# Loading the weights of an attention and MLP kernel in transfers of 88 and 40 partitions instead of 128

## The chip, the cores and the metric

The kernel runs on one core of a Trainium2 chip. The metric is device time in microseconds (us) of one execution; lower is better. The kernel before takes 523.25 us, the median of two runs (522.9 and 523.61).

## The reference

A delta-rule attention of 4 batches, 8 heads, 768 steps and head size 48 is followed by a layer norm and a two-layer MLP (384 to 1536 to 384) with a residual. All inputs are float32.

```python
# q, k, v: (4, 8, 768, 48); beta: (4, 8, 768)
k_n = k / (np.linalg.norm(k, axis=-1, keepdims=True) + 1e-06)
for t in range(S):
    y[:, :, t] = q[:, :, t] @ state                     # per batch and head
    v_old = k_n[:, :, t] @ state
    state += beta[t] * outer(k_n[:, :, t], v[:, :, t] - v_old)
x = y.transpose(0, 2, 1, 3).reshape(4, 768, 384)        # heads side by side
xn = (x - mean) / sqrt(var + 1e-06) * g_ln
out = x + maximum(xn @ w_ch1, 0) @ w_ch2                # (384, 1536), (1536, 384)
```

The MLP's weights reach the kernel as 64-bit floats, seen as pairs of 32-bit words. The kernel turns them into float32 itself: per weight it scales the high and the low word and adds them.

## The kernel before, in words

The sequence is cut into 12 chunks of 64 steps, each for all 32 batch-head pairs. Within a chunk the recurrence becomes matrix products with the inverse of a 64 x 64 triangular matrix. For the first chunk this inverse is made by doubling on TensorE (PE), in `first_inverse` (from line 711): five rounds, each with products E (line 770) that VectorE (DVE) merges (line 775), products Z (line 786), DVE transposes of Z (line 735), and copies of Z back into the tile `xt` on ScalarE (ACT), line 729. Round n's Z waits for the `xt` copies of round n-1. Later chunks take another way (`rows_inverse`), prepared beside the work on the chunk before. The MLP of a chunk is interleaved with the recurrence of the next one: lines 1406 and 1448 or 1426 for the first chunks, lines 1307 and 1523 (a scheme of seven products) from then on.

The weights come in 12 pieces of 128 partitions x 1536 words (768 KB). `fetch` (line 568) loads one piece in two transfers of 384 KB, each 128 partitions x 3 runs of 1 KB, both issued from ACT's queue through the helper `dma` (line 407), so that all issues have line 410. A piece lands in one of five buffers: three tiles `words`, and the two halves of `h_all`, a tile that the MLP needs only later. `convert` (line 579) is an ACT scaling of the high words (line 592), a DVE shift (line 597), an ACT scaling of the low words (line 600) and a GpSimd (POOL) addition (line 610) into `w1_sb` or `w2_sb`.

The order of the work is written out. Every operation is recorded as a numbered step; the text `ORDER` (line 156) lists the steps, `emit` (line 101) issues them in that order, and `in_this_order` (line 25) keeps it on each engine. So each engine carries out a fixed sequence, and an instruction that waits holds up all that follow on its engine. A transfer issued from ACT stands in ACT's sequence among its copies.

The two hardware queues for transfers, SP's and ACT's, share eight completion counters, which the framework hands out in turn to the transfers of both in the order of `ORDER`. An issue waits until the transfer that had its counter before it, eight transfers earlier, has landed. So at most eight transfers of SP and ACT together are in flight. Numbering the transfers from 0, those around the start of the weights are: 9 `kr` and 10 `beta_b`, 11 `v`, 12 `tb`, 13 and 14 `tb` (q), 15 `v`, 16 `kr` (all SP), 17 to 22 weights (ACT), 23 `gd` and 24, 25 `gb` (SP), 26 to 29 weights (ACT), and then again SP's.

Of the kernel before, what the change touches and what calls it, by code (L numbers as in the profile page):

```python
# [53 lines left out]
class Line:  # L54
# [14 lines left out]
    def add(self, eng, cost, fn, r=(), w=(), name="", after=(), **plan):  # L69
        s = Step()  # L70
        s.eng, s.cost, s.fn, s.n, s.name, s.plan = eng, cost, fn, len(self.steps), name, plan
        s.out = w[0] if w else None
        s.opens, s.shuts = [], []
        for k in (*r, *(k for k in w if k in self.unread and k not in r)):
            if k in self.writer:
                self.writer[k].opens.append(k[:2])
                s.shuts.append(k[:2])
        self.unread.difference_update(r)
        self.unread.update(w)
        s.key = f"{self.tag} {eng} {name or next(k if isinstance(k, str) else k[0] for k in w)}"  # L80
        deps = set()
        if eng == "ACT" and "bulk" not in plan and "table" in self.writer:
            deps.add(self.writer["table"])
        for k in r:
            if k in self.writer:
                deps.add(self.writer[k])
        for k in (*w, *after):
            if k in self.writer:
                deps.add(self.writer[k])
            deps.update(self.readers.get(k, ()))  # L90
        for k in r:
            self.readers.setdefault(k, []).append(s)
        for k in w:
            self.writer[k] = s
            self.readers[k] = []
        deps.discard(s)
        s.deps = deps
        self.steps.append(s)
        return s
# [158 lines left out]
def kernel(  # L258
# [13 lines left out]
    nc = tc.nc  # L272
# [98 lines left out]
    add = line.add  # L371
# [18 lines left out]
    def half(e):  # L390
        return slice(C * e, C * e + C)
# [15 lines left out]
    def dma(eng, out_, in_, n, ns, r=(), w=(), **kw):  # L407

        cost = 0.65 if eng != "SP" else 0.45 if n <= 512 else 0.62
        add(eng, cost, lambda: QUEUE[eng].dma_start(out=out_, in_=in_), r, w, bulk=n * ns / 16e3, np=n, **kw)  # L410
# [14 lines left out]
    for i in (2, 1):  # L425
# [6 lines left out]
            out=ident, in_=ident, compare_op=ALU.not_equal, fill=1.0, base=0, pattern=[[-1, 128]], channel_multiplier=1  # L432
# [20 lines left out]
    for n in MASKED:  # L453
        k_, m, w = min(n, 4) if n == 6 else n, masks[n] if n < 6 else mask4, C if n < 6 else BK
# [3 lines left out]
                out=t1, in0=xor[:, 0:w], scalar1=w - 1, scalar2=k_, op0=ALU.bitwise_and, op1=ALU.logical_shift_right  # L458
# [6 lines left out]
                out=t2, in0=own, scalar1=k_, scalar2=1, op0=ALU.logical_shift_right, op1=ALU.bitwise_and  # L465
# [5 lines left out]
                out=m, in0=t1, scalar=1, in1=t2, op0=ALU.is_equal, op1=ALU.mult  # L471
# [20 lines left out]
    for e in range(2):  # L492
        c_pool(
            lambda e=e: nc.gpsimd.affine_select(
                out=pmask[half(e)], in_=pmask[half(e)], compare_op=ALU.is_gt, fill=0.0, base=0,
# [69 lines left out]
    BUF = [3, 4, 0, 1, 2, 0, 1, 2, 0, 1, 2, 0]  # L565
    RUN = 128

    def fetch(i, after=(), **kw):
        dst = words[BUF[i]].rearrange("p n w -> p (n w)").rearrange("p (b a x) -> p a b x", a=2, x=2 * RUN)
        src = pieces[i][1]  # L570
        if len(src.shape) == 2:
            src = src.rearrange("p (a n) -> p a n", a=2)
        for a in range(2):
            dma(
                "ACT", dst[:, a], src[:, a].rearrange("p (b x) -> p b x", x=2 * RUN), 384, 54,
                w=[("wd", BUF[i], a)], after=after, **kw,
            )

    def convert(i, c0=0, n=WN, **kw):

# [1024 lines left out]
    for i in range(5):  # L1605
        fetch(i, pr=-70 + i, after=["keys in"])
# [14 lines left out]
    for c0 in (0, 384):  # L1621
        for i in range(3):
            convert(i, c0, 384, pr=-50 if c0 == 0 else -10)
    fetch(5, pr=-55)
    for i in range(3, 6):
        convert(i, pr=2)
# [27 lines left out]
    for i in range(6, len(pieces)):  # L1654
        fetch(i, pr=i)
        convert(i)
    for i in (2, 3):
        add(
            "Pool", 1.0, lambda i=i: nc.gpsimd.memset(xts[i], 0.0), [], [("xz", i)], pr=20,
            after=[("xt", i, 0), ("xt", i, 1)],  # L1660
# [91 lines left out]
```

## Time and profile before

| | |
|---|---|
| median of two runs | 523.25 us |
| profiled execution | 520.78 us, its span from first to last instruction 519.1 us |
| granted TensorE clock, mean | 0.982 |
| PE busy | 487.1 us (94% of the span) |
| DVE, ACT, POOL busy | 360.8, 206.9, 280.3 us |
| chain that ended last | PE 79%, DMA 5%, SP's queue 3%, issue 3%, DVE 3%, ACT 3% |
| weight transfers | 24 of 384 KB, issued from 10.1 to 83.7 us |
| issue to landing of one, min, median, max | 3.5, 4.5, 7.3 us into `words`; median 7.0 us into `h_all` |

The page gives the busy time of each engine, the span in 40 slices, the chain of work that ended last, and groups of instructions by line. A name like ACTq or SPq is the issuing part of that engine. The timeline lists instructions in order of time: start, duration, engine, line, operation, tiles, count, and in brackets how long the engine had stood idle and what ended that. "issue" is time for which the profile shows no wait. Beside these views the trace has the moments at which a transfer's 16 shares report to its counter; the 16th is its landing.

### The profile page before, as it was taken

How to read it: one execution, taken by the hardware profiler on the slowest of the kernel's cores; microseconds unless marked ns; L12 is line 12 of the kernel's file. 1: busy time of each engine (PE TensorE's matmuls, PEld its weight loads, DVE VectorE, ACT ScalarE, POOL GpSimd, SP SyncE). 2: the span in 40 equal slices, each digit the busy share in tenths (PEclk: the TensorE clock that was granted, in tenths of full speed). 3: DMA queues.
4: the chain of work that ended last, by engine and by line, in shares of the span. 5: the costliest groups of instructions: out<-in, count | busy, mean ns of one | idle time of the engine just before them, and what ended most of it. 6: DMA issues, size and time to landing. Idle time of an engine off the chain costs nothing.

```text
span 519.1 us, 22785 instructions
## 1 busy us (share of the span) xinstructions
PE 487.1 (94%) x9972; PEld 448.9 (86%) x9972; DVE 360.8 (70%) x814; ACT 206.9 (40%) x462; POOL 280.3 (54%) x447
## 2 busy tenths in 40 slices
PE   5577888999899999999999999999999999999997
PEld 4466786768798889999999989999999999999996
DVE  6577739798887567988889986757988446244241
ACT  5587845423431333234242632533513514424130
POOL 3435654604554877976764274473453742564554
PEclk9878998999999999999999999999999999999999
DMA  9957876585515866345853356643404403003011
GB/s 135 294 115 204 191 154 178 107 195 95 90 26 141 156 134 109 68 88 141 167 120 55 83 108 157 132 81 66 102 10 111 104 17 93 4 1 100 2 39 30
DMA packets 181635, 54.56 MB, mean 105 GB/s; under 512 B 164888, under 2 KB 177312, under 8 KB 181536
## 3 DMA queue, kind: packets, MB, share of 16 engines
q1 hardware_dynamic: 168512, 40.10, 37.9%
q10 hardware_dynamic: 10816, 9.83, 6.6%
q0 software_dynamic: 2208, 3.17, 3.8%
q8 instruction: 78, 1.28, 1.0%
q14 instruction: 21, 0.17, 0.1%
HBM read 36.30 MB, written 16.78 MB: 102 GB/s over the span
## 4 chain that ended last, share of the span: by engine, by line
PE 79%; DMA 5%; SPq 3%; issue 3%; DVE 3%; ACT 3%; POOL 2%; ACTq 0%; DVEq 0%; POOLq 0%
PE f L1523 27%; PE f L1307 22%; PE f L1426 6%; PE f L1448 3%; SPq L410 3%; PE two L819 3%; PE by L1033 2%; PE two L1033 2%; PE by L1095 2%; DMA xnt<-xld 2%; PE two L1088 2%; PE f L1406 1%; PE two L1105 1%; DMA words<-in_moe_w_ch_dram 1%; DMA gb<-gd 1%
## 5 line engine op out<-in xcount | busy, mean ns | idle before, releaser
L1510 POOL TENSOR_TENSOR h_all<-h_all 128x256 f32<-128x256 f32 x99 | 72.7, 745 | 30.5 <-PE f L1523 13.8
L1523 PE MATMUL f<-w_sb,h_all 128*128 128x192 f32 x396 | 82.2, 331 | 1.0 <-ACT h_all L1334 0.6
L1523 PE MATMUL f<-words,h_all 128*128 128x192 f32 x396 | 76.7, 329 | 0.0
L1523 PEld LDWEIGHTS f<-w_sb,h_all 128*128 128x128 f32 x396 | 65.1, 190 | 3.0 <-ACT h_all L1334 1.6
L1330 DVE TENSOR_TENSOR h_all<-f,h_all 128x512 f32<-128x512 f32 x72 | 48.9, 685 | 26.4 <-PE f L1307 19.3
L1523 PEld LDWEIGHTS f<-words,h_all 128*128 128x128 f32 x396 | 65.0, 190 | 1.5 <-issue 0.5
L1548 POOL TENSOR_TENSOR words<-h_all 128x128 f32<-128x128 f32 x66 | 31.2, 491 | 63.4 <-ACT h_all L1334 30.4
L907 DVE TENSOR_TENSOR tmp<-xb,gb 128x31 f32<-128x31 f32 (+19 forms) x139 | 57.5, 413 | 3.9 <-POOL xb L894 0.3
L1325 ACT COPY h_all<-f 128x512 f32<-128x512 f32 x45 | 26.2, 586 | 82.4 <-PE f L1307 68.8
L914 DVE TENSOR_TENSOR xb<-xb,tmp 128x31 f32<-128x31 f32 (+19 forms) x139 | 52.6, 378 | 3.7
L410 POOL DMA_DIRECT2D tb<-in_k_dram x64 | 42.2, 662 | 0.3 <-POOL tb L1630 0.3
L1334 ACT ACTIVATE h_all<-h_all 128x512 f32<-128x512 f32 x54 | 32.7, 626 | 23.9 <-DVE h_all L1330 23.5
L1307 PE MATMUL f<-x_new,w_sb 128*128 128x128 f32 x288 | 40.3, 278 | 0.1
L1307 PE MATMUL f<-xnt,w_sb 128*128 128x128 f32 x288 | 40.2, 277 | 0.0
L1307 PEld LDWEIGHTS f<-x_new,w_sb 128*128 128x128 f32 x288 | 36.5, 191 | 0.6 <-issue 0.2
L1307 PEld LDWEIGHTS f<-xnt,w_sb 128*128 128x128 f32 x288 | 36.5, 192 | 0.6 <-issue 0.2
L1541 DVE TENSOR_TENSOR o<-f,x 128x192 f32<-128x192 f32 x33 | 11.4, 352 | 36.8 <-PE f L1523 30.9
L1426 PE MATMUL f<-xnt,w_sb 128*128 128x256 f32 x144 | 34.5, 387 | 1.4 <-issue 1.4
L1426 PEld LDWEIGHTS f<-xnt,w_sb 128*128 128x128 f32 x144 | 26.4, 190 | 5.4 <-issue 1.8
L1523 PE MATMUL f<-w_sb,words 128*128 128x192 f32 x132 | 26.3, 329 | 0.0
L682 POOL TENSOR_TENSOR v<-v,kpair 128x768 f32<-128x768 f32 x10 | 14.7, 1473 | 14.0 <-DVE pt L897 14.0
L610 POOL TENSOR_TENSOR w_sb<-words 128x768 uint32<-128x768 uint32 (+1 forms) x11 | 14.7, 1348 | 13.7 <-ACT words L600 10.2
(239 smaller groups left out, 983.4 us busy)
## 6 DMA issues: line engine op xcount, KB each, us to landing
words<-in_moe_w_ch_dram ACTq DMA_DIRECT2D x20, 384.0 KB, 4.5
gd<-gsb SPq DMA_DIRECT2D x11, 512.0 KB, 3.9
v<-in_v_dram SPq DMA_DIRECT2D x24, 192.0 KB, 4.2
kr<-in_k_dram SPq DMA_DIRECT2D x46, 96.0 KB, 3.4
out_dram<-o SPq DMA_DIRECT2D x46, 96.0 KB, 2.2
xld<-xlt SPq DMA_DIRECT2D x9, 384.0 KB, 2.4
xnt<-xld SPq DMA_DIRECT2D x36, 96.0 KB, 2.9
tb<-in_q_dram SPq DMA_DIRECT2D x40, 64.0 KB, 2.8
```

The lines of the kernel that those rows point to most:

```text
L410: add(eng, cost, lambda: QUEUE[eng].dma_start(out=out_, in_=in_), r, w, bulk=n * ns / 16e3, np=n, **kw)
L907: lambda j=j, n=n, w=w, t=t: nc.vector.tensor_tensor(out=t, in0=xv[:, 0:n, j : j + 1].to_broadcast([128, n, w]), in1=gv[:, j : j + 1, j + ...
L914: "DVE", dve(n * w), lambda t=t, rest=rest: nc.vector.tensor_tensor(out=rest, in0=rest, in1=t, op=ALU.subtract),
L1033: nc.tensor.matmul(dst[half(e), hp, j], src[drows(hp), (e if n else key_half(c, hp, e)) * GP + j], s_all[drows(hp), e, j], start=(n == 0 o ...
L1307: nc.tensor.matmul(wide(p[:, f : f + 128]), w[:, f : f + 128], r, start=start and i == 0, stop=True, skip_group_check=True)
L1325: add("ACT", act(512), lambda: nc.scalar.copy(o, p), pk, ok)
L1330: add("DVE", dve(512), lambda: nc.vector.tensor_tensor(out=o, in0=x, in1=y, op=op), [*xk_, *yk], ok)
L1334: add("ACT", act(512), lambda: nc.scalar.activation(o, o, ACTF.Relu, scale=scale), [], ok)
L1426: nc.tensor.matmul(p[:, 0:TOK], w1_sb[:, t, f * 128 : (f + 1) * 128], xnt[:, t], start=(t == 0), stop=(t == KC - 1))
L1510: add(eng, cost, lambda: e.tensor_tensor(out=out_, in0=x, in1=y, op=op), r, w, port=2 if eng == "Pool" else 1, pr=-2)
L1523: lambda f=f, t=start and f == order[0]: nc.tensor.matmul(p[:, 0:D2], lhs(f), rhs[:, f], start=t, stop=(f == order[-1]), skip_group_check=True
L1548: lambda f=f + i: e.tensor_tensor(out=s3[f], in0=one(0, 0)[0](f), in1=one(1, 0)[0](f), op=ALU.subtract),
```

## The change

Each of the 24 weight transfers is issued as two, partitions 0 to 87 and partitions 88 to 127, one right behind the other on ACT's queue. Bytes, runs, buffers, the recorded steps and `ORDER` stay as they are: one step now issues two transfers.

```diff
+        def go(a):
+            for r in (slice(0, 88), slice(88, 128)):
+                nc.scalar.dma_start(out=dst[r, a], in_=src[r, a].rearrange("p (b x) -> p b x", x=2 * RUN))
+
         for a in range(2):
-            dma(
-                "ACT", dst[:, a], src[:, a].rearrange("p (b x) -> p b x", x=2 * RUN), 384, 54,
-                w=[("wd", BUF[i], a)], after=after, **kw,
-            )
+            add("ACT", 1.3, lambda a=a: go(a), after, [("wd", BUF[i], a)], bulk=384 * 54 / 16e3, np=384, **kw)
```

The cost (1.3) and the other numbers given to `add` were for a planner and do not act here, since the order is written out. Each of the 48 transfers takes a counter in turn, so from the first weights on each transfer up to the last weights has another counter and another predecessor than before; behind the last weights the turn is the same again, since 24 is a multiple of eight.

## The prediction

> **What bounds the kernel now.** I read the page first, then a table by stretches, then the chain and ACT's timeline over the time in which weights are issued (10.1 to 83.7 us).
>
> ```profile
> PE   5577888999899999999999999999999999999997
> q10 hardware_dynamic: 10816, 9.83, 6.6%
> q8 instruction: 78, 1.28, 1.0%
> words<-in_moe_w_ch_dram ACTq DMA_DIRECT2D x20, 384.0 KB, 4.5
> h_all<-in_moe_w_ch_dram ACTq DMA_DIRECT2D x4, 384.0 KB, 7.0
> ```
>
> The first seven slices of 13 us are the only ones in which PE is not full, and weights move only there. What is lost there moves all that follows; nothing behind can take it back, since each engine's order is fixed.
>
> ```profile
> 10.00:30.00 20.00, 13.54 (x411) 11.46 (x413) 11.03 (x23) 12.50 (x32) 5.86 (x10) 0.81 0.98 231
> 30.00:50.00 20.00, 15.55 (x600) 13.44 (x596) 15.79 (x40) 15.18 (x34) 10.89 (x15) 0.84 0.77 172
> 100.00:519.00 419.00, 410.52 (x7750) 383.98 (x7742) 293.41 (x627) 143.75 (x315) 232.93 (x380) 1.00 0.43 89
> ```
>
> Columns are length, busy time of PE, PE's weight loads, DVE, ACT, POOL, granted clock, share of the DMA engines, GB/s. From 10 to 30 us the DMA engines are full (0.98) while no computing engine is: this is the inverse of the first chunk, one short operation after another. From 100 us on PE works 410.52 of 419 us.
>
> The chain of work in that stretch, start, duration and what:
>
> ```profile
> 20.65 0.69 PE two L770 x30
> 21.34 0.38 PE by L628 x2
> 21.72 2.54 issue
> 24.26 1.54 PE by L628 x6
> 25.80 1.96 PE f L786 x64
> ```
>
> PE stands still for 2.54 us although no wait is recorded, and only then does round 2's product Z (line 786, 25.80) come. This product needs the copies into `xt` that ACT makes meanwhile:
>
> ```profile
> 17.53 0.50 ACTq L410 DMA_DIRECT2D h_all<-in_moe_w_ch_dram  x1
> 17.71 0.20 ACT L674 COPY knat<-knrm 64x8 f32<-64x8 f32 x1
> 18.73 0.37 ACT L729 COPY xt<-f 128x256 f32<-128x256 f32 x1 [0.82 <-DVE qt L735]
> 19.08 0.38 ACTq L410 DMA_DIRECT2D h_all<-in_moe_w_ch_dram  x1
> 19.55 0.74 ACT L729 COPY xt<-f 64x256 f32<-64x256 f32 x2 [0.45 <-DVE qt L735]
> 20.69 0.75 ACT L729 COPY xt<-f 64x256 f32<-64x256 f32 x2 [0.39 <-DVE qt L735]
> 21.25 0.38 ACTq L410 DMA_DIRECT2D words<-in_moe_w_ch_dram  x1
> 21.46 0.37 ACT L729 COPY xt<-f 64x256 f32<-64x256 f32 x1
> ```
>
> The copies end at 21.83, so they have 25.80 - 21.83 = 3.97 us to spare. Weight issues stand between them. The waits of SP's queue show that an issue does wait for its counter's earlier transfer:
>
> ```profile
> SPq L410 <- DMA words<-in_moe_w_ch_dram: 12.0, 6, 2.7
> ```
>
> **The change, part by part.** It removes nothing. It adds 24 issues on ACT's queue and gives the transfers of both queues other predecessors, as the turn of eight goes faster. Times below are on the profile's own scale; that execution took 520.78 us, 2.5 below the median of 523.25, and I add the difference in time to the median.
>
> *Issue time.* Weight issues one behind the other start 0.42 and 0.54 us apart (16.57, 16.99, 17.53), so an added one costs ACT's queue about 0.45, all 24 about 11 us. What counts is where a copy that the chain needs stands behind it.
>
> *First piece, 10.05 us.* The copy of `kt` (line 633) that starts at 10.51, right behind the issue, comes 0.45 later, and through the product of line 695 (11.66) the whole chain to 17.17. The next two issues stand before gaps of ACT (0.79 us at 14.31). The second of 14.43 has transfer 14 (`tb`) before it, landed at 16.29 by its counter; its issue ends at 16.7, where the copy behind it started at 16.6. Value **+0.45**, already spent inside the spare time of the next step.
>
> *`h_all`, the step that matters.* Before, the three issues at 16.57, 16.99 and 17.53 had transfers 12 to 14 before them, all landed by 16.29. Now they are six. The first gets the counter of transfer 15 (`v`, issued 10.21, to landing 9.2 us in the view of that tile, so 19.42), the second that of 16 (`kr`, landed 20.06 by its counter), the others those of the first two pieces. ACT's queue stands until 19.42, issues the second at 20.06, and four more at 0.45: the first `xt` copy starts at about 22.0 instead of 18.73. Behind it stands the fourth `h_all` transfer, now two, with the counters of the second and third of those six, issued at 20.1 and 20.5. To landing I take 5 us, between the page's median of 4.5 and the 5.9 of the fastest into `h_all`: 25.1 and 25.5. The second is issued by 25.9, the remaining five copies take 1.9 us without a gap (0.74 + 0.75 + 0.37; DVE's transposes are long done), and they end at 27.9. Z of round 2 starts there instead of at 25.80: **+2.1**. PE's standstill of 2.54 us is cover here; without it Z could have started at 23.3 (25.80 - 2.54), and these waits would cost 4.6. From below: `v` and `kr` land 0.8 and 1.0 us earlier, since the `h_all` transfers no longer compete with them, and the landings take the smallest of 3.5 us: copies end near 25.2, nothing lost. From above: 8.1 us, the most into `h_all`: end near 31, +5.2.
>
> *First `words1` piece, 29.14 and 29.55 us.* Two issues become four; behind them stands an `xt` copy on which round 3's Z waits (line 786 at 30.94, released by ACT's line 729). Their predecessors (a weight transfer, `gd`, two `gb`) have landed by then with the same shift. **+0.9**; between 0.8 and 1.1 by the two distances above.
>
> *SP's queue.* `gd`, `gb`, `kr` now have the weights of 14.43 to 29.55 before them. The last `gb` waits for the last part of `words1`, issued near 33 and landed near 38 to 39; before it waited until 36.12. The same 3 us, not added to the others: `kr` behind it is needed at 43.79, by which time PE is that much later too.
>
> *The other 16 added issues* (42.47 to 83.70 us). By my walk along the turn their predecessors have landed; the nearest is `tb` under the issue at 43.83, less than 2 us early. ACT has gaps there (1.59 us at 48.80, 0.85 at 50.12, 1.0 to 1.6 us five times from 69 to 80) and runs behind PE. I take **+0.3**, for the four at 42 to 45 us, where ACT has little rest. Bounds: 0, and 16 x 0.45 = 7.2 if every gap were on the chain.
>
> *Bandwidth.* No byte is added. A transfer of `words` issued alone lands after 3.5 us, so from both sides: nothing, or what the rival on fewer engines gives.
>
> The Trainium skill's page "DMA: Bandwidth & Descriptors", under "Rules for kernel authors", advises against two transfers to disjoint partition halves: they share the same engines and serialize. By that rule the split brings nothing to set against the issues, as the sum has it; no run so far shows it.
>
> **Sum**: 2.1 + 0.9 + 0.3 = 3.3 us, so 523.25 + 3.3 = **526.5 us**, 0.6% slower.
>
> **The rivals.**
> *Fewer engines.* 88 and 40 partitions may not spread over all 16 engines. A packet takes 6.6% x 16 x 519.1 us / 10816 = 51 ns; over 16 engines a transfer is 24 packets (1.2 us) each, if 88 run on eleven engines with 8 partitions each and 40 on ten with 4 (both divide so), 12 partitions and 36 packets on the busiest (1.8 us). With four to five pairs ahead of the landing that the fourth `h_all` transfer waits for, it comes 0.6 x 4 = 2.5 us later: 529. For it: the engines are full from 10 to 30 us. Against: while ACT stands, less is in flight.
> The same page, under "Why a DMA increments its semaphore by 16 and not by 1", states that a transfer uses the largest number up to 16 that divides its slowest dimension, hence 11 and 10, the lowest-numbered. By it the sum would be 529 in the crowd; the trace of before, with all its transfers in multiples of 16, cannot show it.
>
> *Faster: PE's standstills go.* PE stands 2.54 us (21.72) and 1.72 us (83.95) on the chain with no wait shown, both while weights are in flight, and q8 moves 78 blocks of 16 KB (1.28 MB / 78) of instructions. If those queue behind weight packets and the split leaves the engine that brings them free, both standstills can go, and landings come early. The first saves nothing unless the `xt` copies are also ready; so 523.25 - 1.7 + 0.9 + 0.3 - up to 1.5 (waits resolved by 24.3) = about 521 to 523. Against: the bound of 25.2 on the copies leaves 0.6 at most. It decides if round 2's Z starts before 25.
> The Trainium skill, "Runtime: NRT & Kernel Launch", section "Instruction fetch mechanics", has sequencers refill in 16 KB blocks over a DMA queue, mostly hidden; the block size agrees with q8, the standstills speak against "hidden".
>
> *Hidden.* Landings are quick and the 3.97 us of spare cover the wait: 0.9 + 0.3, 523.5 to 524.5.
>
> *A wait chain.* One late landing in the turn of eight holds ACT, whose next issues are the predecessors of the next: SP and ACT wait for each other through 50 us. For it: SP already loses 12 us to weights. With the upper bounds, 5.2 + 1.1 + some 3 of the 7.2: 532 and more.
>
> **How the numbers follow.** Forecast (524.5 to 528) 0.50; fewer engines (528 to 531) 0.18; hidden 0.13; faster 0.11; wait chain 0.08. The range 522 to 531 leaves out the wait chain and half of "faster". A measurement of this kernel tells about 2% (10.5 us) from no change: slower beyond 533.7 is part of the wait chain, 0.05; faster beyond 512.8 needs more than all standstills, 0.01; within 0.94.
>
> **What would show it.** In ACT's timeline six `h_all` issues, the first near 19.4, then a standstill until two more near 25, with `xt` copies of line 729 behind them near 22 and 26; Z of line 786 near 28; four `words1` issues in a row. From 100 us on everything moved by one constant. Wrong would be: `h_all` issues not waiting, a shift that grows behind 50 us, or Z before 25.

## The result, and the profile after

The changed kernel takes **531.39 us** (median of two runs, 531.12 and 531.67) against 523.25: 8.1 us more, a ratio of **1.0156 [1.0112, 1.0199]**. That is within the 2% that tells a change from none by the yardstick used here, but above the forecast of 526.5 and just above the range of 522 to 531. Here and below a ratio leaves out executions over 1.5% above the fastest of their kernel, and is not the quotient of the two medians.

The profiled execution took 531.67 us (span 530.0), 10.9 more than that of before. These two numbers differ from the medians because single executions of one and the same kernel scatter by about 1% here (before: 517 to 529 us in all batches together), and the profile of before shows one of the quicker ones. So shifts between two profiles are read below only with other profiles of the same arrangement beside them.

The page of the changed kernel (lines of code are one higher than before), in this order: PE's busy share in 40 slices, the queue of the weights, the queue of instructions, the weight transfers, and the chain's shares by engine:

```profile
PE   4757698899989999999999999999999999999997
q10 hardware_dynamic: 10936, 9.83, 7.3%
q8 instruction: 78, 1.28, 1.1%
words<-in_moe_w_ch_dram ACTq DMA_DIRECT2D x20, 264.0 KB
PE 71%; DMA 9%; DVE 4%; POOL 4%; ACT 4%; issue 3%; SPq 3%; ACTq 2%; DVEq 0%; POOLq 0%
```

Bytes are the same (9.83 MB), packets nearly so. What is new is in the last line: ACT's issuing part holds 2% of the chain, 0% before, and transfers 9% instead of 5%. In the slices the loss again lies in the first eight. The table by stretches (columns as before):

```profile
10.00:30.00 20.00, 13.48 (x306) 11.35 (x306) 9.15 (x20) 7.66 (x20) 5.86 (x10) 1.00 0.97 182
30.00:50.00 20.00, 15.55 (x515) 13.86 (x516) 13.54 (x31) 16.41 (x39) 7.86 (x11) 0.67 0.79 142
100.00:519.00 419.00, 413.36 (x7996) 384.74 (x7995) 299.11 (x637) 151.44 (x331) 233.24 (x377) 1.00 0.43 91
```

From 10 to 30 us ACT works 7.66 us instead of 12.50: it stands. The granted clock is 1.00 there and 0.81 before, so the clock is not the reason. ACT's timeline around the `h_all` issues shows what it stands for:

```profile
19.71 5.37 ACTq L575 DMA_DIRECT2D h_all<-in_moe_w_ch_dram  x6
25.18 0.37 ACT L730 COPY xt<-f 128x256 f32<-128x256 f32 x1 [6.41 <-DMA h_all<-in_moe_w_ch_dram]
27.79 1.40 ACTq L575 DMA_DIRECT2D h_all<-in_moe_w_ch_dram  x2
29.29 0.74 ACT L730 COPY xt<-f 64x256 f32<-64x256 f32 x2 [3.73 <-DMA h_all<-in_moe_w_ch_dram]
29.67 0.30 ACTq L575 DMA_DIRECT2D words<-in_moe_w_ch_dram  x1
30.05 1.14 ACT L730 COPY xt<-f 64x256 f32<-64x256 f32 x3
```

Six issues in a row, the first at 19.71; ACT's copies idle 6.41 us before the first `xt` copy; then 3.73 us more behind the second group. PE's timeline has the other end of it:

```profile
25.36 0.88 PE L629 MATMUL by<-ident,tb 128*128 128x128 f32 x6 [0.46 <-issue]
30.90 2.42 PE L787 MATMUL f<-xt,gsb 64*64 64x64 f32 x64 [4.66 <-issue]
```

Round 2's Z starts at 30.90 (25.73 before), behind a standstill of 4.66 us.

To see at which place the time goes, I follow one and the same ACT instruction through all profiles: how much later than in the profile of before it starts, for instructions that stood at 43, 80 and 100 us there and for one near the end.

| us later than in the profile of before | at 43 | at 80 | at 100 | at 505 |
|---|---|---|---|---|
| the change | 6.5 | 13.7 | 11.5 | 10.8 |
| the change, another execution | 6.6 | 12.4 | 9.8 | 11.8 |

From 100 us on the shift stays within 2 us, as forecast. But only about half of it is there at 43 us; the rest comes between 43 and 80 us, where the forecast had 0.3 us. A shift that grows behind 50 us is one of the signs that the prediction itself named as wrong: from 50 to 80 us it goes from 6.6 to 13.7 us, and from 8.0 to 12.4 in the other execution.

Two theories come out of this. **Front**: the turn of the eight counters, with the six issues behind `v` and `kr`. **Late**: something in the 14 later transfers, either the time of their issues on ACT's queue, or slower landings because 88 and 40 partitions use fewer engines. The experiments take the two places apart, then the causes within each.

### The profile page after: what moved, and what is told of

Same layout as the page of the kernel before. It is cut to its first block, busy times and chain, and to the rows that moved or that the text cites. A ratio compares the mean times of both kernels' runs of the same rounds, so it can differ in the third digit from the quotient of the medians.

```text
span 530.0 us, 22834 instructions
## 1 busy us (share of the span) xinstructions
PE 492.7 (93%) x9972; PEld 455.2 (86%) x9972; DVE 362.1 (68%) x814; ACT 206.6 (39%) x462; POOL 279.8 (53%) x447
## 3 DMA queue, kind: packets, MB, share of 16 engines
q10 hardware_dynamic: 10936, 9.83, 7.3%
## 4 chain that ended last, share of the span: by engine, by line
PE 71%; DMA 9%; DVE 4%; POOL 4%; ACT 4%; issue 3%; SPq 3%; ACTq 2%; DVEq 0%; POOLq 0%
PE f L1524 26%; PE f L1308 22%; PE f L1427 6%; DMA words<-in_moe_w_ch_dram 4%; PE two L820 3%; SPq L410 3%; PE f L1449 2%; ACTq L575 2%; PE by L1034 2%; PE two L1089 2%; PE by L1096 2%; PE two L1034 2%; PE two L1106 1%; DMA gd<-gsb 1%; DMA gb<-gd 1%
## 5 line engine op out<-in xcount | busy, mean ns | idle before, releaser
L1335 ACT ACTIVATE h_all<-h_all 128x512 f32<-128x512 f32 x54 | 32.8, 626 | 24.0 <-DVE h_all L1331 23.8
L1308 PE MATMUL f<-xnt,w_sb 128*128 128x128 f32 x288 | 40.3, 278 | 0.0
L1542 DVE TENSOR_TENSOR o<-f,x 128x192 f32<-128x192 f32 x33 | 11.5, 351 | 35.4 <-PE f L1524 30.0
L1407 PE MATMUL f<-xnt,w_sb 128*128 128x128 f32 x144 | 21.4, 312 | 3.6 <-ACT h_all L1415 3.6
```

What stands on the lines that cost most here:

```text
L1308: nc.tensor.matmul(wide(p[:, f : f + 128]), w[:, f : f + 128], r, start=start and i == 0, stop=True, skip_group_check=True)
L1335: add("ACT", act(512), lambda: nc.scalar.activation(o, o, ACTF.Relu, scale=scale), [], ok)
L1407: nc.tensor.matmul(p[:, 0:128], w1_sb[:, t, f * 128 : (f + 1) * 128], xnt[:, t, cols], start=(t == 0), stop=(t == KC - 1))
```

## The experiments

Every ratio is against the kernel before, run beside it (523.58, 523.35 and 523.59 us in the three groups), with its 95% interval.

### The changed kernel once more

No edit; it stands beside `first`, `last` and `s8048`.

> The changed kernel itself (88 and 40 partitions everywhere), for an interval and as the yardstick beside the other three. Every theory: 1.5% slower than before, 530 to 532 us; in the profile round 2's product Z (line 787) near 31 us instead of 25.8, everything behind 100 us moved by 9 to 11 us.

Measured: 532.93 us, **1.0202 [1.0107, 1.0296]**, a little above what was expected. Together with the first measurement the change costs 1.6 to 2.0%. This and what follows is the yardstick for the parts.

### Splitting only the first five pieces, only the last seven

```diff
-            for r in (slice(0, 88), slice(88, 128)):
+            for r in (slice(0, 88), slice(88, 128)) if i < 5 else (slice(0, 128),):    # "first"
+            for r in (slice(0, 88), slice(88, 128)) if i >= 5 else (slice(0, 128),):   # "last"
```

The first five pieces are the ten transfers up to 36 us, the last seven the 14 from 42 us on.

> Only the first five pieces split (10 added issues, all before 40 us), the other seven as before. Theory 'two places': the front loses 5 to 6 us by ACT standing for counters and the late issues lose 3 to 4 on their own, so 528 to 529.5 us here, with Z of round 2 near 31. Rival 'one place': all of it is lost in the front and the later growth follows from it: 531 us. Rival 'given back': the shift of the front is absorbed by 60 us, and the loss is the late issues': 523 to 525 us.

> Only the last seven pieces split (14 added issues, from 42 us on), the first five as before. Theory 'two places': nothing moves before 42 us, then the added issues on ACT's queue cost 2.5 to 4 us, 526 to 527 us. Rival 'one place': 523 to 524 us. Rival 'given back': 530 to 531 us.

Measured: first **1.0071 [1.0018, 1.0124]**, last **1.0101 [1.0058, 1.0144]**. Each costs something; the sum, 1.7%, is what the whole costs. So there are two losses in two places that add up, and the late one, which I had put at 0.3 us, is about as large as the front (late 5.3 us by its ratio and 3.0 by the difference of the medians of the group, front 3.7 and 3.2). The median of `last`, 526.56 us, is where "two places" had it; that of `first`, 526.82, is below its 528 to 529.5, so the front costs less than the 5 to 6 us expected.

Where the late one arises shows in the chain of `last`, followed back through the time of its late issues (start, duration, what; steps of up to 0.05 us left out):

```profile
76.22 0.47 ACTq L575
76.69 0.43 issue
77.11 0.80 ACTq L575
77.96 0.07 ACT nrm_b L884
78.07 0.31 ACTq L575
78.39 0.56 issue
78.95 0.80 ACTq L575
79.80 0.28 ACT h_all L1415
...
84.41 0.80 ACTq L575
85.24 0.84 ACTq L575
86.11 0.80 ACTq L575
86.96 0.29 ACT h_all L1415
```

The chain runs from issue to issue on ACT (L575), with ACT's short copies between them; an issue that lies on it whole takes 0.80 to 0.84 us. PE waits for these copies: its products of line 1407 follow at 81.90 and 87.29. In `first`, whose late transfers are whole, the chain of the same stretch belongs to PE's products, and no issue is on it:

```profile
77.20 1.44 PE f L945 x84
78.65 2.88 PE f L1407 x24
81.52 1.39 PE by L950 x103
82.91 2.90 PE f L1407 x24
```

### The second part of the late transfers issued from SP

```diff
+            for r in (slice(0, 88), slice(88, 128)) if i >= 5 else (slice(0, 128),):
-                nc.scalar.dma_start(out=dst[r, a], ...)
+                (nc.sync if r.start else nc.scalar).dma_start(out=dst[r, a], ...)
```

The 14 late transfers are split as in `last`, with the same counters in the same turn and the same sizes. Only who issues the 40-partition part differs.

> Only the last seven pieces split, at 88 and 40, but the 40-partition part is issued from SP's queue, so that ACT has as many issues as before; the turn of counters and the engines used stay as in the run with both parts on ACT (526.6 us). Theory 'issue time on ACT's queue': the loss of 3 us goes, 523 to 524.5 us, with the shift of the h_all copies of line 1415 from 60 to 80 us under 2 us. Rival 'engines and late landings': it stays, 526 to 527 us. If SP's own order is what is hurt (its issues then wait for free buffers between the q loads), it is 528 or more.

Measured: 521.47 us, **0.9987 [0.9950, 1.0024]**, against 1.0101 [1.0058, 1.0144] for `last`: the whole late loss is gone, and the intervals do not meet. It is even under the 523 to 524.5 us that "issue time on ACT's queue" had. Fewer engines per transfer and the faster turn of counters are both still there, so neither of them by itself is the late loss; it comes with the second issue on ACT's queue. (The issue of the 88-partition part that is left to ACT takes 0.84 us late, a whole one 0.55: 4 us more over the 14 than before the change, and they cost nothing that shows beyond the interval.) The chain of this kernel, again followed back through the late issues:

```profile
77.28 7.29 DMA words<-in_moe_w_ch_dram
84.58 0.01 issue
84.59 5.28 DMA words<-in_moe_w_ch_dram
89.88 0.00 issue
89.88 0.91 ACT words L601
```

No issue of ACT's is on it. One thing moves together with the issue time: in `last` the transfers that ACT issues late are also the predecessors for which SP's queue waits. SP's waits for weights, from the table of waits (sum, count, longest), first of `last`:

```profile
SPq L410 <- DMA words<-in_moe_w_ch_dram: 32.1, 6, 12.9
```

and of the kernel with the second part on SP:

```profile
SPq L410 <- DMA words<-in_moe_w_ch_dram: 12.5, 6, 4.2
```

12.5 us is as much as before the change (12.0). So the run shows that the time of the issues on ACT is where the loss begins. That PE loses much of it to ACT's late copies can be read in all profiles, from the time for which its products of line 1407 wait for these copies between 50 and 105 us: 2.8 to 4.1 us in the five with both parts of 88 and 40 from ACT (the change, `again`, `last`, and two of a kernel below), 1.6 to 2.6 us in three with parts of 80 and 48 from ACT (below), 1.2 here and 1.6 in the last kernel below, 0.7 in the kernel before, and none in the other three with whole late transfers. How much SP's late transfers add behind that, the runs don't separate.

### 80 and 48 partitions instead of 88 and 40

```diff
-            for r in (slice(0, 88), slice(88, 128)):
+            for r in (slice(0, 80), slice(80, 128)):
```

Both parts are multiples of 16, so this tells the number of engines apart from the number of issues. It shortens the late issues as well (0.57 and 0.62 us instead of 0.83 and 0.80), so in the late stretch it cannot tell engines from issue time. It was run for all pieces, twice, and for the first five and the last seven alone (with the conditions on `i` shown above).

> Split at 80 and 48 instead of 88 and 40: the same 48 issues and the same turn of counters, but both sizes divide by 16. Theory 'fewer engines': part of the loss is that 88 and 40 run on 11 and 10 engines, so the load of kr that the second h_all issue waits for lands near 20 to 21 us instead of 23, Z of round 2 starts near 28 instead of 31, issue to landing after 70 us falls from 5.2 to about 4.7, and the time is 526 to 528 us. Rival 'turn and issues alone': how many engines carry a transfer does not matter; kr lands near 23 again, Z near 31, 530 to 532 us.

> 80 and 48 everywhere once more, since its first time came from four executions, and its profile had a long stretch at half clock from 46.5 to 67 us. By the parts (front 1 to 2 us, late part 2.5 to 3.5): 527 to 529 us. If the engines make no difference: 531 to 533 us, as with 88 and 40.

> Only the first five pieces split, at 80 and 48, beside the same with 88 and 40 (526.8 us, 0.7% over before). Theory 'fewer engines make the standing long': the second h_all issue waits until 21 us instead of 23, Z of round 2 comes about 2 us earlier, and the loss falls from 3.5 to 1 to 2 us: 524.5 to 525.5 us. Rival 'turn alone': 526.5 to 527.5 us.

> Only the last seven pieces split, at 80 and 48 (all 16 engines), beside the run with 88 and 40 there (526.6 us, 1.0% over before). Theory 'engines matter late too': issues after 66 us take 0.67 us instead of 0.86 and landings come sooner, and the loss falls to about half, 524.5 to 525.5 us. Rival 'number of issues alone': 526 to 527 us.

| split | all pieces | first five | last seven |
|---|---|---|---|
| 88 and 40 | 1.0156 [1.0112, 1.0199]; 1.0202 [1.0107, 1.0296] | 1.0071 [1.0018, 1.0124] | 1.0101 [1.0058, 1.0144] |
| 80 and 48 | 1.0162 [1.0081, 1.0243]; 1.0083 [1.0042, 1.0123] | 1.0048 [1.0012, 1.0084] | 1.0074 [1.0020, 1.0127] |

Three of the four are a little lower with 80 and 48 (one, 1.0162, is not), but the intervals of every pair overlap. The times don't tell the two apart; splitting costs with all 16 engines as well. Alone, the first five (526.47 us) and the last seven (526.57 us) came where the rivals had them, for which the engines don't matter; of the two times for all pieces, 529.98 is just under the rival's range and 527.8 in the theory's.

The traces do tell them apart, in two things. First the reports: a transfer of 88 partitions (issued at 48.63 us in the changed kernel) reports once at 49.11 and eleven times from 51.95 to 54.08; its other half once at 49.56 and ten times from 52.66 to 54.59. Parts of 80 and 48 report 16 times. That is the rule of the Trainium skill, "DMA: Bandwidth & Descriptors", section "Why a DMA increments its semaphore by 16 and not by 1" (the largest number up to 16 that divides the partitions: 11 and 10), and the trace agrees. Second, the landing of `kr`, on which the `h_all` issues stand:

| profile | `kr` landed | round 2's Z | round 3's Z |
|---|---|---|---|
| whole transfers in front (before; last; last8048; lastsp) | 20.1; 20.3; 20.5; 20.1 | 25.7; 27.9; 28.8; 28.4 | 31.0; 32.7; 33.6; 33.7 |
| 80 and 48 (s8048; s8048_b; first8048) | 21.0; 21.8; 21.3 | 28.1; 28.2; 29.2 | 33.8; 33.9; 36.2 |
| 88 and 40 (the change; again; first) | 23.1; 22.2; 23.4 | 30.9; 30.0; 30.3 | 36.6; 36.2; 35.9 |

In the four profiles of the next two experiments, whose Z does not compare, `kr` landed at 20.3 with whole transfers and at 22.8, 23.4 and 21.4 with 88 and 40. So on the mean it lands 2.5 us later beside parts on 11 and 10 engines and 1.1 us later beside parts on 16, though the two ranges overlap (21.4 to 23.4 and 21.0 to 21.8). And the first row shows how quick the front of the profile of before was: the other three whole fronts have their Z 2.2 to 3.1 us later. Against those, Z of the change (30.0 to 30.9) is late by 1 to 3 us, not by 5.

### The `h_all` issues moved behind the copies

```diff
 ORDER
-... 208 90 92 91 46 ... 109 251 258 112 ... 138 135 89 137 136 131 129-130 141-143 ...
+... 208 46 ... 109 112 ... 138 135 137 136 131 129-130 90 92 91 89 251 258 141-143 ...
```

Steps 90, 92, 91 and 89 are the `h_all` transfers; they now stand behind round 1's `xt` copies, for which round 2's Z waits. 251 and 258 are SP's first two `gb`, moved along. Once in the changed kernel (twice run), once in the kernel before (`hlater128`).

> The changed kernel (88 and 40 everywhere), with the eight h_all issues moved in ORDER behind the last xt copy of round 1 (and the steps of the first two gb transfers behind them, so that gd and gb keep their place on SP's queue). Nothing else differs. Theory 'ACT stands for counters': the xt copies no longer stand behind the h_all issues, so they end near 24 us instead of 31; round 2's Z starts near 26 to 27 instead of 31, most of the 5 us of the front come back, and the time is 526 to 528 us against 533 with the issues in their old place. Rival 'bytes in the crowd': the same transfers on 11 and 10 engines hold up the loads and the instruction refills wherever they are issued; Z near 30, 531 us or more.

> The kernel with 88 and 40 everywhere and the h_all issues behind round 1's xt copies once more: its first time (530.4 us, four executions from 525.8 to 533.3) was wider than its profile, in which the front had lost nothing against the runs with an unsplit front. Theory 'standing for counters, plus issue time late': what stays is the late loss alone, as in the run with only the last seven pieces split: 526 to 528 us. Rival 'the move returns nothing': 530 to 532 us, as the changed kernel.

> The same move of the h_all issues in the kernel before (transfers of 128 partitions). Every theory: these issues did not hold the xt copies up there, so little changes, 522 to 525 us. If it is under 521, the crowd of transfers itself costs the front and the kernel before can be bettered.

Measured: in the changed kernel **1.0122 [1.0040, 1.0204]** and **1.0119 [1.0058, 1.0179]**; in the kernel before 520.77 us, **0.9941 [0.9906, 0.9976]**, which beats both kernels of this case and is under the 522 to 525 us that every theory had. The changed kernel with the move (530.39 and 528.96 us) lies between its theory (526 to 528) and its rival. So the move gains 0.6% without any split, and in the changed kernel hardly more (1.2% is left of 1.6 to 2.0%). Between the two moved kernels the split costs 1.8%, as much as it did before the move: the standing ahead of the `xt` copies, which the move takes away, is not by itself what the split costs. ACT's timeline of the moved and split kernel shows why:

```profile
23.60 2.96 ACTq L578 DMA_DIRECT2D h_all<-in_moe_w_ch_dram  x6
26.61 0.55 ACT L596 ACTIVATE words<-words 128x384 f32<-128x384 f32 x1 [2.96 <-DMA h_all<-in_moe_w_ch_dram]
28.60 0.90 ACTq L578 DMA_DIRECT2D words<-in_moe_w_ch_dram  x2
29.60 1.07 ACT L637 COPY qt<-by 128x512 f32<-128x512 f32 x2 [2.44 <-DMA h_all<-in_moe_w_ch_dram]
```

and PE's timeline of the same kernel:

```profile
24.65 1.18 PE L790 MATMUL f<-xt,gsb 64*64 64x64 f32 x64
30.73 0.58 PE L774 MATMUL by<-qt,gsb 64*64 64x64 f32 x9 [4.89 <-ACT qt L637]
```

Z comes at 24.65, earlier than before the change (25.73), and then PE waits 4.89 us (in the other execution 26.82 and 3.83) for the `qt` copies, which now stand behind issues whose counters are still taken. The standing has moved to the next copies. Without the split the same copies run at 24.31.

### Both cures at once

The moved order, and the second part of the late transfers from SP:

```diff
-                nc.scalar.dma_start(out=dst[r, a], ...)
+                (nc.sync if r.start and i >= 5 else nc.scalar).dma_start(out=dst[r, a], ...)
```

> 88 and 40 everywhere, with both costs taken away: the h_all issues behind round 1's xt copies, and from the sixth piece on the 40-partition part issued from SP's queue. Theory 'two places': nothing of the loss is left, 521 to 524.5 us. Rival 'fewer engines cost by themselves': 526 us or more.

Measured: **1.0053 [1.0023, 1.0083]**. The time, 525.69 us, lies between "nothing of the loss is left" (up to 524.5) and the rival (526 or more): the two cures together don't take the whole loss away. Against the moved kernel with both parts from ACT (1.0119 and 1.0122) it is 0.7% lower, by intervals that still meet. Against the moved kernel with whole transfers (0.9941) 1.1% are left. That would be the front's cost, and it agrees with `first` by its interval (0.2 to 1.2%).

The shifts of all profiles beside each other, as in the table above:

| us later than in the profile of before | at 43 | at 80 | added on the way | time on the way at granted clock 0.5 |
|---|---|---|---|---|
| late parts 88 and 40, both from ACT: the change; again; last; hlater; hlater_b | 6.5; 6.6; 3.3; 3.4; 4.1 | 13.7; 12.4; 7.2; 7.7; 12.1 | 7.2; 5.8; 3.9; 4.3; 8.0 | 8.0; 10.2; 1.0; 1.3; 17.1 |
| late parts 80 and 48, both from ACT: s8048; s8048_b; last8048 | 3.7; 3.9; 4.7 | 10.2; 8.6; 5.6 | 6.5; 4.7; 0.9 | 20.4; 6.8; 0.5 |
| second part from SP: lastsp; both | 3.0; 3.9 | 1.6; 4.7 | -1.4; 0.8 | 3.4; 5.1 |
| late transfers whole: first; first8048; hlater128 | 4.9; 5.4; -0.2 | 6.0; 6.7; -1.1 | 1.1; 1.3; -0.9 | 3.4; 3.4; 0 |

The late stretch loses 3.9 to 8.0 us wherever ACT issues both parts of 88 and 40, and -1.4 to 1.3 us wherever it issues one. Some of this goes with the granted clock, which falls to 0.5 for a while in every profile (3.4 us on this way in that of before): the three largest losses of the first row have 8.0 to 17.1 us of it, and the three profiles with 80 and 48, which don't agree, stand in its order. But `last` and `hlater` lose 3.9 and 4.3 us with 1.0 and 1.3 us of it, while `lastsp` and `first` have -1.4 and 1.1 with 3.4. Part is also given back behind 80 us: counted to the instruction at 100 us, `last` and `hlater` have lost 2.6 and 2.9 us, and the profiles with one late issue from ACT -0.5 to 2.1.

## Why the prediction failed

**The step that failed is "The other 16 added issues", with +0.3.** `last` costs 1.0% (5.3 us by its ratio, 3.0 by the medians) where 0.3 us, under 0.1%, was forecast; with the second part issued from SP this cost is gone. (The number was wrong too: 14 of the added issues are behind 42 us.) Two things in it were off. The size: I took 0.45 us for an added issue from the front. Late, an issue of the change took 0.82 us, and those of before already 0.50 to 0.56:

| mean us of one issue | up to 40 us | 40 to 66 | from 66 on | sum from 40 us on |
|---|---|---|---|---|
| before | 0.42 | 0.50 | 0.56 | 7.5 (14 issues) |
| the change | 0.38 | 0.71 | 0.82 | 21.6 (28 issues) |
| 80 and 48 in all pieces (s8048; s8048_b) | 0.47; 0.50 | 0.58; 0.58 | 0.67; 0.63 | 17.8; 16.9 (28 issues) |

ACT's queue gets 14 us more, not 16 x 0.45 = 7.2. So even the upper bound was taken from the wrong rows. The rows of the right stretch stood in the profile of before (0.55 us each from 69 us on), but they would have given 14 x 0.55 = 7.7; that a part takes 0.82 stands in no row of before. The cover: "ACT has gaps there" was read off the timeline of before, gap by gap. But the gaps are ACT's waits for PE's products (8.1 us in ten waits for line 1406 from 50 to 100 us), and PE in turn needs ACT's small copies of line 1414. Before, it waited for them once, 0.7 us; in `last` three times, 3.8 us. An issue put there does not just fill a gap, it stands ahead of the next copy; the chain of `last` above goes from issue to issue. Bounds of 0 and 7.2 were written down, and the value was put next to the lower one with no row to say that those gaps were spare.

**Issue time in the first piece, +0.45 hidden**: right in kind. The `kt` copy came 0.81 later (11.32 after 10.51), and this vanishes in the standing behind it.

**`h_all`, +2.1**: what ACT does came point by point. The first of six issues waited for `v` (forecast 19.4, 19.71 measured, `v` landed at 19.69), the second for `kr`, the next group for the landing of the second and third of the six. The times were late by what `kr` was late: it landed at 23.07, not at 20.06. The first copy came at 25.18 (forecast 22.0), the next group at 27.79 (25), Z at 30.90 (27.9). So of the rivals, "fewer engines" named a delay of this size (2.5 us), but at another link: I had put it on the landing ahead of the fourth `h_all` transfer, it was `kr`, issued among the first split weights. That the front as a whole still cost only what was forecast (0.7%, 3.7 us by its ratio, forecast 2.1 + 0.9 = 3.0) is partly luck: Z at 28 is what whole transfers give in three other executions, so the 25.80 I counted from was early.

**`words1`, +0.9**: from round 2's Z to round 3's it takes 5.7 to 6.2 us with 88 and 40 in front, 4.8 to 5.2 with whole transfers. The size is right. The reason was not: "their predecessors have landed" fails for the third of the four. ACT's timeline of the change:

```profile
34.71 0.30 ACTq L575 DMA_DIRECT2D words<-in_moe_w_ch_dram  x1
35.05 0.92 ACTq L575 DMA_DIRECT2D words<-in_moe_w_ch_dram  x1
36.47 0.74 ACTq L575 DMA_DIRECT2D words<-in_moe_w_ch_dram  x2
37.25 0.36 ACT L730 COPY xt<-f 64x256 f32<-64x256 f32 x1 [1.65 <-DMA words<-in_moe_w_ch_dram]
```

It starts at 36.47, 0.02 us after a `gb` of SP's had landed.

**SP's queue, not added**, was too small: `gd` went from 19.51 to 24.41, 4.9 us instead of 3, and the last `gb` from 36.12 to 43.37, 7.3 us instead of 3. SP's waits for weights went from 12.0 to this, in the table of waits of the change:

```profile
SPq L410 <- DMA words<-in_moe_w_ch_dram: 45.2, 13, 15.2
```

This is the mutual waiting of the rival "wait chain", and it does hang on the counters. In the front it is even what the chain of the change goes through, from a weight transfer to SP's `gd` and `gb` and back to ACT's issue, and not Z (steps of up to 0.05 us left out):

```profile
15.52 8.81 DMA words<-in_moe_w_ch_dram
24.41 6.90 DMA gd<-gsb
31.32 5.13 DMA gb<-gd
36.47 0.30 ACTq L575
36.81 6.54 DMA words<-in_moe_w_ch_dram
```

`first` has the same chain; that of `again` goes over `kr`, the `h_all` issues and the `qt` copies of line 634. So the two paths end close together, and which of them sets the front's loss is not settled. That the turn of the counters by itself carried the loss through 50 us is not what the runs show: with the second part issued from SP, the turn is the same and the late loss is gone.

**Bandwidth, and the rule on two partition halves** (the Trainium skill, "DMA: Bandwidth & Descriptors", "Rules for kernel authors"): no run with a split was faster than its unsplit counterpart beyond its interval, so the traces agree that it brings nothing. **Faster** fell by its own sign, Z before 25. The standstill that it was built on did shrink: ahead of the same products of line 628 (629 in the change) PE stood 2.54 us before, 0.46 in the change and less than 0.15 in `again` and `first`, against 3.30 to 3.83 in the three other whole fronts. Nothing was gained, since 4.0 to 4.7 us without a recorded wait now stand behind these products, directly ahead of Z, while ACT is held from the copies that Z needs. Why the first standstill shrank, no run shows. **Hidden** fell with ACT's timeline: the copies end at 31.2, behind anything that 3.97 us of spare could cover.

What stays open: in the front, how much of the 0.7% is the turn of the counters and how much the later landing of `kr`, and by which of the two paths it reaches PE. The landmarks differ by 1 to 2 us between 80/48 and 88/40, the times (1.0048 and 1.0071) can't tell. Also open is why an issue of 88 or 40 partitions takes longer late than early.

## What to carry to other kernels

An issue on an engine's queue is work of that engine: price it by the duration that issues have in the very stretch where it will stand, and call a gap spare only if the instruction behind it is not what the bounding engine waits for. Where two issuing queues share completion counters in turn, look for where a standing goes: here moving the issues away from one copy moved it to the next, and giving the added issues to the other queue took the late cost away. Before taking differences of two profiles apart, get a second profile of each, since one quick execution can hide or double a term of 3 us.

## What was not expected of the hardware

- **The length of an issue depends on how the partitions are cut and on the time.** From 66 us on a whole transfer took ACT 0.55 us (median), parts of 80 and 48 took 0.57 and 0.62, parts of 88 and 40 took 0.83 and 0.80. Early on most parts of 88 or 40 took 0.29 to 0.40 us, no longer than a whole transfer (0.37 to 0.50); three of the twenty in the change took 0.64 to 0.92. SP took 0.76 us (median) for a part of 40, from 43 us on.
- **A part of 88 or 40 partitions reports to its counter long before its data lands**: once, 0.5 to 0.7 us after most of the short issues begin and 1.2 to 1.3 us after those of 0.8 us, and then 11 or 10 times as the data lands, 3 to 7 us after the issue from 48 us on. That the early report makes up the 16 fits these counts; the trace gives no amounts.
- **The granted clock falls to 0.5 for stretches of 3 to 20 us that lie elsewhere in each execution**: 22.6 to 32.8 us in the profile of before, 30.2 to 40.4 in that of the change, 20.5 us from 46.5 on in that of 80 and 48. The scatter of 1% between executions goes along with it. Of the 69 executions of the kernel before in the three groups, the 16 with the highest mean clock (0.984 and more) took 521.0 us on the mean, the 16 with the lowest (0.974 and less) 525.5. Which of the two causes the other, no run separates.
